# A spectral filter and a GEGLU block, forward and backward: the first W sums in two stretches, transposes a step earlier, the tail first in its step, a third Vt slot

## The chip, the cores and the metric

The kernel runs on one core of a Trainium2 chip. The metric is the device time of one execution in microseconds, as the median of several runs. A separate execution was recorded by the hardware profiler. All traces and rows below come from that one.

PE is the tensor engine (matmul), DVE the vector engine, ACT the scalar engine, POOL the GpSimd engine, and SP the engine whose queue issues most DMAs. PSUM is the memory into which PE writes its sums.

## The reference, cut to what matters

```python
x = A_x                                   # 2048 x 576
g = sigmoid((x * gate_w).sum(-1, keepdims=True))
a = irfft2(rfft2(x) * (A_w_r + 1j * A_w_i))
b = (gelu(x @ W_gate) * (x @ W_up)) @ W_down      # 576 -> 4608 -> 576
out = g * a + (1 - g) * b
# returned: out, and for a given grad_out the gradients of
# x, A_w_r, A_w_i, W_gate, W_up, W_down and gate_w
```

All inputs and outputs are bf16. The forward product `b` is needed as well as its gradients, so every intermediate of the GEGLU block is formed once and used several times.

## The kernel before, in words

**Layout.** The 2048 rows of x and of grad_out are held as 16 row tiles of 128 rows. `xn` and `dB` hold them by rows, `xT` and `dOT` transposed. The 4608 hidden columns are cut into 18 groups of 256 (`FG`). The first stage loops over groups `g` and, inside, over `m` = 0 to 3, each `m` being four row tiles. One pass of the inner loop is called a step here, numbered `pr` = 4g + m (0 to 71).

**What one step does.** `H_mm` makes z = dOT x W_down^T (lines 402 and 407) and the two 64-row parts of xy (line 411). The inner function `full` adds the main part of xy = xT x [W_gate, W_up] (line 418) for two row tiles at a time. ACT evacuates z as `da` (L430) and xy as `xb`, `q` and `hu` (L437 to L440). On DVE, `H_ew1` computes the first half of the elementwise work (L445 to L447). `H_ew2` (called through `sigs`) has two sigmoids on ACT (L461, L462) and eight DVE products (L466 to L473) that end in the tiles `A`, `dHu` and `dHg`, 128 x 4 x 256 each. They are stored to DRAM for the second stage and also kept in SBUF.

**W sums.** When a group is through all its 16 row tiles, its weight gradients are summed over them during the next group's four steps. `W_units(g)` returns five lists of closures with a weight in us each: four lists for the four steps, and one that is carried into the step after. `w[0]` to `w[3]` are the gradients of W_gate (k = 1, from `dHg`, `w[0]` and `w[1]`) and W_up (k = 2, from `dHu`), each over 256 of the 576 rows in two halves `cc` of 16 matmuls (L525). `tail` is the last 64 rows of both (L538). `d[0]` to `d[3]` are the gradient of W_down, two halves of 8 matmuls each (L508). Each sum needs one `wps` tile, and there are two such PSUM tiles (pool `pw`). The finished sum is copied out by `wevac` (L486), through ACT or, while `wcopy` is DVE's copy, through DVE. It lands in a stage tile (`dw`, `dwt` or `dwd`, two slots each) and is stored by POOL's DMA queue.

**The spectral part.** The transforms are cut into small units in a list `fft`. `want(pr)` says how many of them should have been issued after each step. The table `FIRST` gives this for steps 0 to 7, and from there the rest is spread evenly up to step 65. In a step with n new units, the first sits inside the second half of xy, and the others at points of the W closures where the sum of weights passes a value of `spots`. A unit that finds no such point is issued after the last closure. Units and `z` share one PSUM tile (pool `pz`, one buffer): a unit's matmuls write it, ACT evacuates it, and then the next unit or the next z may write. A forward unit of the first kind is six matmuls (L568), of the second kind two (L585). The second kind and the middle units end in a tile `Vt` of the pool `half` (two slots), stored by an SP DMA (L592, L771).

**Tables.** `build_R` (DVE, L164 and L165), `columns_B` (DVE L180 to L182, then POOL L186 and L189) and `build_B` (POOL iotas L216 to L220, later DVE L225 to L231) prepare tables. Their sines are run on ACT by `run_late` in two steps (`tables`), and in those steps the W sums that come later are copied out by DVE. `scale_dB` scales `dB` in place on DVE (L946) before the `d` sums use it.

**The first group.** For g = 0 nothing is left over from a group before. Instead, the row tiles are transposed by PE as they are needed. `titems` returns three closures per source and per four row tiles: eight, eight and four transposes (L367 and L373) into a PSUM tile `pg` (two buffers), each followed by a copy into `dOT` or `xT` (L374). `gate` computes the sigmoid gate (L383 to L387) and uses a `pg` buffer too. `held` delays the second elementwise half of a step into the next step.

**Order.** The schedule is manual: each engine executes its instructions in the order in which the program text issues them. An instruction that waits holds everything behind it on its engine.

**The second stage**, from about 960 us, reads the stored tiles back transposed and forms `b` and the gradient of x (L1140).

Of the kernel before, what the change touches and what calls it, by code (L numbers as in the profile page):

```python
# [11 lines left out]
BF16 = mybir.dt.bfloat16  # L12
# [8 lines left out]
P, T = 128, 16  # L21
# [9 lines left out]
FG = 256  # L31
TPB = 512 // FG
# [212 lines left out]
def kernel(  # L245
# [4 lines left out]
    nc = tc.nc  # L250
# [7 lines left out]
    unit = Unit(ctx.enter_context(tc.tile_pool(name="unit", bufs=NUNIT, side="right")), "unit")  # L258
    hstack = ExitStack()
    hres = hstack.enter_context(tc.tile_pool(name="hres", bufs=1, side="right"))  # L260
    half = Unit(hstack.enter_context(tc.tile_pool(name="half", bufs=2, side="right")), "half")
    wpool = hstack.enter_context(tc.tile_pool(name="wpool", bufs=2, side="right"))

    wstack = ExitStack()
# [220 lines left out]
    def wevac(out, in_):  # L485
        wcopy[0](out, in_)  # L486

    def W_units(g):
        fsl = slice(g * FG, (g + 1) * FG)
        kt = kept[g]  # L490

        def tl(k, t):
            return kt[t // 4][k][:, t % 4, :]
        dwd_tiles, wp = {}, {}

        def halves(f, us):
            return [(us, lambda: f(0)), (us, lambda: f(1))]

        def wtile(key):
            if key not in wp:  # L500
                wp[key] = pw.tile([P, TPB, FG], F32, tag="wps", name="wps")
            return wp[key]

        def u_dwd(fch, h):
            def f(half):
                wps = wtile(("d", fch, h)).rearrange("p a b -> p (a b)")
                for t in range(8 * half, 8 * half + 8):
                    nc.tensor.matmul(wps[:, :288], lhsT=tl(0, t)[:, fch * P:(fch + 1) * P],  # L508
                                     rhs=dB[:, t, h * 288:(h + 1) * 288], start=(t == 0), stop=(t == T - 1))
                if half == 0:  # L510
                    return
                if h == 0:
                    dwd_tiles[fch] = stage.tile([P, D], BF16, tag="dwd", name="dwd")
                dwd = dwd_tiles[fch]
                wevac(dwd[:, h * 288:(h + 1) * 288], wps[:, :288])
                if h == 1:
                    r0 = g * FG + fch * P
                    wst[0].dma_start(out_6[r0:r0 + P, :], dwd[:])
            return halves(f, 1.0)

        def u_dw(k, ov, c0):
            def f(cc):
                wps = wtile(("w", k, c0))
                for t in range(T):
                    nc.tensor.matmul(wps[:, cc, :], lhsT=xn[:, t, (c0 + cc) * P:(c0 + cc + 1) * P],  # L525
                                     rhs=tl(k, t), start=(t == 0), stop=(t == T - 1))
                if cc == 0:
                    return
                dw = stage.tile([P, TPB, FG], BF16, tag="dw", name="dw")
                wevac(dw[:], wps[:])  # L530
                wst[0].dma_start(ov[:, c0:c0 + TPB, fsl], dw[:])  # L531
            return halves(f, 1.7)

        def tail():
            wps = wtile("t")
            for t in range(T):
                for k, r in ((1, LO), (2, HI)):
                    nc.tensor.matmul(wps[r, 0, :], lhsT=xn[:, t, 512:576], rhs=tl(k, t),  # L538
                                     start=(t == 0), stop=(t == T - 1))
            dw = stage.tile([P, FG], BF16, tag="dwt", name="dwt")  # L540
            wevac(dw[:], wps[:, 0, :])
            wst[0].dma_start(out_4[512:576, fsl], dw[LO, :])
            wst[0].dma_start(out_5[512:576, fsl], dw[HI, :])
        tl_ = [(2.0, tail)]
        w = [u_dw(k, ov, c0) for k, ov in ((1, o4v), (2, o5v)) for c0 in range(0, 4, TPB)]
        d = [u_dwd(fch, h) for fch in range(FCH) for h in range(2)]
        if g == 0:
            return [[w[0], tl_], [w[1], d[0]], d[1:], [w[2]], w[3]]
        return [[d[0]], [d[1], d[2], d[3]], [w[0], tl_], [w[1], w[2]], w[3]]


    side = []
# [356 lines left out]
    mid_at = 4 * T + 10  # L909
    NPR = NT // 2  # L910
    LASTP = NG * NPR - 7
    FIRST = (0, 0, 0, 0, 0, 3, 5, 9)
    done = [0]

    def want(pr):
# [22 lines left out]

    wgT_from = 54

    carry, pend, held = [], None, []
    scaled = [0]

    def scale_dB(n):
# [4 lines left out]
    for g in range(NG):  # L949
# [3 lines left out]
        for m in range(NPR):  # L953
            pr = g * NPR + m
            n = want(pr) - done[0]
            done[0] += n
            hs = [h for u in pend[m] for h in u] if pend else []

            def side_work(us):
                while side and us > 0:  # L960
                    us -= side[0][0]
                    side.pop(0)[1]()
            tiles = [ewt(tag, g) for tag in ("xb", "q", "hu")]
            state = []

            def sigs(m=m, tiles=tiles, state=state):
                H_ew2(g, m, tiles, state[0], state[1])
            if g == 0:
                pgs3 = (pgtile,) * 3
                if m < NPR - 1:  # L970
                    t1 = 4 * m + 4
                    cp = ((VC, VC, VC), (VC, VC, VC)) if m == 0 else ((VC, VC, AC), (AC, VC, VC))
                    its = titems(dB, dOT, t1, pgs3, cp[0]) + titems(xn, xT, t1, pgs3, cp[1])
                else:
                    its = []
                z, xy_full = H_mm(g, m, [lambda: gate(0)] if m == 0 else its[:2])
                da = H_da(g, m, z)
                if m > 0:
                    for f in its[2:]:
                        f()  # L980
                if held:
                    held.pop()()
                xy = xy_full(0)
                if m == 0:
                    for f in its:
                        f()
                    build_R(nc, tb, unit, 4)
                    columns_B(nc, tb, res)
                    next(makeB)
                for part in (1, 0):  # L990
                    H_act(0, xy, tiles, part)
                xy = xy_full(1)
                for part in range(2):
                    H_act(1, xy, tiles, part)
                if m < NPR - 1:
                    gate(m + 1)
                state += [H_ew1(g, tiles), da]
                if m < NPR - 1:
                    held.append(sigs)
                else:  # L1000
                    V.tensor_copy(g32[:], g_bf[:])
                    V.tensor_scalar(gs32[:], g32[:], SD2, None, op0=ALU.mult)
                    sigs()
            else:
                z, xy_full = H_mm(g, m)
                xy = xy_full(0)
                da = H_da(g, m, z)
                for part in (1, 0):
                    H_act(0, xy, tiles, part)
                xy = xy_full(1, fft_next if n else None)  # L1010
                for part in range(2):
                    H_act(1, xy, tiles, part)
                state += [H_ew1(g, tiles), da]
                if pr == 4:
                    scale_dB(12)
                elif pr == 5:
                    scale_dB(4)
                    build_R(nc, tb, unit, 8)
                    build_R(nc, tb, unit, 12)
                elif pr == 6:  # L1020
                    next(makeB)
                side_work(4.4)
                at, k = 0.0, min(n, 1)
                spots = (0.0, 1.6, 3.6) if n < 4 else (0.0, 1.0, 2.6, 4.2, 5.0, 5.0)
                tables = pr in (4, 6)
                for w, f in carry + hs:
                    if k < n and at >= spots[k - (n == 2)]:
                        fft_next()
                        k += 1
                    if tables and k == n:  # L1030
                        run_late(tb)
                        wcopy[0] = VC
                        tables = False
                    if pr == NG * NPR - 1 and at == 0.0:
                        sigs()
                    f()
                    at += w
                wcopy[0] = AC
                while k < n:
                    fft_next()  # L1040
                    k += 1
                flush()
                if pr < NG * NPR - 1:
                    sigs()
            carry = []
            if m < 3 and g + 1 < NG:
                load_w(g + 1, m)
            if done[0] == n_slots or (pr >= wgT_from and pr % 2 == 0 and len(wgT_all) < 20):
                load_wgT()
                if done[0] == n_slots:  # L1050
                    load_wgT()
# [243 lines left out]
```

## Time and profile before

| what | value |
|---|---|
| median of 3 runs | 1433.06 us (1432.56 to 1434.38) |
| the profiled execution | 1435.61 us |
| its span, first to last instruction | 1433.8 us |
| mean granted clock of PE | 0.994 |
| PE busy | 1380.7 us (96%) |
| DVE busy / ACT busy | 735.9 us (51%) / 731.4 us (51%) |
| POOL busy | 222.6 us (16%) |
| start of z in steps 1, 2, 3, 4 | 20.39, 30.80, 44.22, 50.28 us |
| start of z in steps 5, 6, 7, 8 | 70.73, 84.00, 98.99, 112.43 us |

How to read the rows: a timeline row gives start, duration, engine, line and operation, output <- inputs, tile shape and how many instructions were merged, and in brackets how long the engine had been idle before it and what released it. A row of waits gives who waited for whom, the total, how often and the longest. In the 40 slices of the page a digit is the busy share in tenths. PEclk is the clock that PE was granted, in tenths of full speed.

### The profile page before, as it was taken

Reading aid. Unit: us, or ns where it says so; the run is one execution under the profiler, and the core shown is the slowest. Engines: PE = TensorE matmul, PEld = TensorE weight load, DVE = VectorE, ACT = ScalarE, POOL = GpSimd, SP = SyncE. Lnnn points to the kernel's source line nnn. Section 1 sums busy time; section 2 is a strip of 40 time slices with the busy share of each in tenths; the row PEclk is TensorE's granted clock in tenths of the full one; section 3 lists DMA queues with packets and bytes.
Section 4 is the critical chain, followed back from the end, with each engine's and each line's share of the span. In section 5 each row is a group of like instructions: output and inputs, shape, how many; then the busy total and the mean of one; then the engine's idle time right before and its main releaser. Section 6 shows DMA issues by size and latency. Waiting matters only on the chain.

```text
span 1433.8 us, 28098 instructions
## 1 busy us (share of the span) xinstructions
PE 1380.7 (96%) x11357; PEld 1026.5 (72%) x11430; DVE 735.9 (51%) x1403; ACT 731.4 (51%) x1324; POOL 222.6 (16%) x420
## 2 busy tenths in 40 slices
PE   8799999999999899999999999999999999999997
PEld 6466766766766666667767676768777777777775
DVE  7775656464887688784665656551000642212100
ACT  6777777677778788777677777662000000000000
POOL 3000010122344236330100010110000100000000
PEclk9899999999999999999999999999999999999999
DMA  6333344445564565555356554859999997788772
GB/s 210 96 85 110 107 120 120 120 124 151 130 162 126 138 162 141 143 149 155 104 155 166 132 154 131 179 128 228 212 193 198 235 202 167 157 159 167 157 155 61
DMA packets 509534, 214.62 MB, mean 150 GB/s; under 512 B 311418, under 2 KB 502588, under 8 KB 509404
## 3 DMA queue, kind: packets, MB, share of 16 engines
q1 hardware_dynamic: 493402, 187.44, 55.8%
q0 software_dynamic: 13872, 24.24, 6.2%
q8 instruction: 89, 1.46, 0.5%
q10 hardware_dynamic: 2130, 1.15, 0.3%
q14 instruction: 41, 0.34, 0.1%
HBM read 41.05 MB, written 93.84 MB: 94 GB/s over the span
## 4 chain that ended last, share of the span: by engine, by line
PE 92%; ACT 3%; DVE 2%; DMA 1%; issue 1%; SPq 0%; ACTq 0%; DVEq 0%
PE acc L1140 29%; PE wps L525 18%; PE xy L418 16%; PE z L402 9%; PE wps L508 9%; PE wps L538 2%; PE xy L411 2%; PE pf L568 2%; PE z L407 2%; PE pf L838 1%; PE pf L840 1%; PE pf L677 1%; PE pf L766 1%; PE pf L812 1%; PE pf L585 1%
## 5 line engine op out<-in xcount | busy, mean ns | idle before, releaser
L1140 PEld LDWEIGHTS <-pin 128*128 128x128 bf16 x3456 | 337.7, 98 | 86.3 <-DMA pin<-scr 1.1
L418 PE MATMUL xy<-wgu,xT 128*128 128x512 bf16 x1079 | 257.7, 381 | 10.3 <-issue 9.6
L525 PEld LDWEIGHTS <-xn 128*128 128x128 bf16 x2304 | 225.7, 98 | 44.2 <-issue 6.1
L418 PEld LDWEIGHTS <-xT 128*128 128x128 bf16 x1152 | 106.8, 98 | 138.4 <-issue 31.7
L1157 ACT COPY bo<-acc 128x288 f32<-128x288 f32 x32 | 12.8, 399 | 305.0 <-PE acc L1140 305.0
L466 DVE TENSOR_TENSOR xb<-xb,s 128x1024 bf16<-128x1024 bf16 x72 | 49.8, 692 | 216.0 <-ACT s L462 216.0
L508 PE MATMUL wps<-dB,A 128*128 128x288 bf16 x1152 | 154.8, 286 | 1.9 <-DVE dwd L486 1.9
L402 PE MATMUL z<-wdT,dOT 128*128 128x256 bf16 x1152 | 137.5, 272 | 13.5 <-ACT ev L844 3.0
L1140 PE MATMUL acc<-wgT,pin 128*128 128x288 bf16 x1152 | 143.8, 286 | 0.0
L1140 PE MATMUL acc<-wuT,pin 128*128 128x288 bf16 x1152 | 143.6, 286 | 0.1
L1140 PE MATMUL acc<-wd_all,pin 128*128 128x288 bf16 x1152 | 142.9, 286 | 0.1
L525 PE MATMUL wps<-dHg,xn 128*128 128x256 bf16 x1152 | 137.0, 275 | 5.8 <-DVE dHg L473 5.8
L525 PE MATMUL wps<-dHu,xn 128*128 128x256 bf16 x1152 | 135.8, 273 | 0.0
L508 PEld LDWEIGHTS <-A 128*128 128x128 bf16 x1152 | 112.0, 98 | 32.7 <-issue 2.1
L402 PEld LDWEIGHTS <-dOT 128*128 128x128 bf16 x1152 | 111.4, 98 | 32.9 <-issue 19.1
L531 POOL DMA_DIRECT2D out_dram<-dw x67 | 49.2, 734 | 513.1 <-ACT dw L486 418.5
L430 ACT ACTIVATE da<-z,omg 128x256 bf16<-128x256 f32 x288 | 112.2, 471 | 12.0 <-PE z L407 11.9
L439 ACT CAST xb<-xy 128x512 bf16<-128x512 f32 x144 | 85.2, 592 | 35.0 <-PE xy L418 35.0
L1217 DVE SCALAR_TENSOR_TENSOR f32t<-gwf,dlog,b16t 128x576 f32<-128x576 f32 x16 | 13.1, 818 | 171.4 <-DMA b16t<-dxa_scr 171.4
L437 ACT ACTIVATE q<-xy 128x512 bf16<-128x512 f32 x144 | 88.1, 614 | 8.7 <-PE xy L418 6.8
L486 ACT CAST dw<-wps 128x512 bf16<-128x512 f32 x71 | 41.6, 586 | 90.9 <-PE wps L525 86.8
L440 ACT CAST hu<-xy 128x512 bf16<-128x512 f32 x144 | 87.3, 606 | 0.0
(212 smaller groups left out, 1698.7 us busy)
## 6 DMA issues: line engine op xcount, KB each, us to landing
scr<-A SPq DMA_DIRECT2D x72, 256.0 KB, 2.8
scr<-dHg SPq DMA_DIRECT2D x72, 256.0 KB, 2.9
scr<-dHu SPq DMA_DIRECT2D x72, 256.0 KB, 3.5
out_dram<-dw POOLq DMA_DIRECT2D x67, 128.0 KB, 2.3
wd_all<-in_B_w_down_dram SPq DMA_DIRECT2D x3, 1728.0 KB, 15.9
out_dram<-dwd POOLq DMA_DIRECT2D x34, 144.0 KB, 3.0
scr_p<-Vt SPq DMA_DIRECT2D x32, 145.0 KB, 2.7
wgu<-in_B_w_gate_dram SPq DMA_DIRECT2D x18, 256.0 KB, 4.0
```

The source lines that it names most:

```text
L402: nc.tensor.matmul(zo(t), lhsT=dOT[:, ci, t, :], rhs=wdT[:, ci, :], start=(t % 4 < 2 and ci == 0), stop=False)
L418: nc.tensor.matmul(xy[k][:, t % 2, :], lhsT=xT[:, ci, t, :], rhs=wgu[:, ci, :], start=False, stop=(ci == 3))
L430: nc.scalar.activation(da[:, t, :], z[:, t % 2, t // 2, :], ACT.Copy, scale=omg32[:, 4 * m + t:4 * m + t + 1])
L437: nc.scalar.activation(q[:, h, :], xy[:, :, 0:FG], ACT.Square)
L439: nc.scalar.copy(xb[:, h, :], xy[:, :, 0:FG])
L440: nc.scalar.copy(hu[:, h, :], xy[:, :, FG:2 * FG])
L466: V.tensor_tensor(xb[:], xb[:], s[:], op=ALU.mult)
L486: wcopy[0](out, in_)
L508: nc.tensor.matmul(wps[:, :288], lhsT=tl(0, t)[:, fch * P:(fch + 1) * P], rhs=dB[:, t, h * 288:(h + 1) * 288], start=(t == 0), stop=(t == ...
L525: nc.tensor.matmul(wps[:, cc, :], lhsT=xn[:, t, (c0 + cc) * P:(c0 + cc + 1) * P], rhs=tl(k, t), start=(t == 0), stop=(t == T - 1))
L531: wst[0].dma_start(ov[:, c0:c0 + TPB, fsl], dw[:])
L1140: nc.tensor.matmul(acc[:, :288], lhsT=src[:, r, :], rhs=w_of(r)[:, h * 288:(h + 1) * 288], start=(first and r == 0), stop=(last and r == F ...
```

## The change

- For group 0, the two W_gate sums `w[0]` and `w[1]` are cut at row tile 12: all four stretches over row tiles 0 to 11 are issued in step 4, the four over row tiles 12 to 15 in step 5. Both `wps` tiles stay open in between. In every other group a sum is cut into quarters of 8 matmuls in the same order as before, so that weights are 0.85 instead of 1.7.
- Step 5 also takes the tail of group 0, ahead of `d[0]`. In the later groups the tail goes ahead of `w[0]` in its step. Its stage tile now has the tag `dw` and shares those two slots.
- In group 0, the transposes of dB's row tiles 8 to 11 move from step 1 into step 0, and those of dB's row tiles 12 to 15 from step 2 into the end of step 1 (the last of the three closures into step 2's z). Those of xn stay in their steps, after `da`. Which copies go to ACT and which to DVE changes too.
- The second elementwise half of step 3 is held into step 4, between the first and the second evacuation of xy.
- `build_R(4)` moves from step 0 to step 4, `columns_B` and the first part of `build_B` from step 0 to step 5, `build_R(8)` and `build_R(12)` from step 5 to steps 6 and 7, and the sines from steps 4 and 6 to steps 5 and 7. `scale_dB` does 8 and 8 row tiles in steps 4 and 5 instead of 12 and 4.
- `FIRST` is (0, 0, 0, 0, 0, 0, 3, 5) instead of (0, 0, 0, 0, 0, 3, 5, 9).
- The pool `half` has three slots.

```diff
-    half = Unit(hstack.enter_context(tc.tile_pool(name="half", bufs=2, side="right")), "half")
+    half = Unit(hstack.enter_context(tc.tile_pool(name="half", bufs=3, side="right")), "half")
...
-        def u_dw(k, ov, c0):
-            def f(cc):
+        def u_dw(k, ov, c0, cut=T // 2):
+            both = cut != T // 2
+
+            def f(cc, t0, t1):
                 wps = wtile(("w", k, c0))
-                for t in range(T):
+                for t in range(t0, t1):
                     nc.tensor.matmul(wps[:, cc, :], lhsT=xn[:, t, (c0 + cc) * P:(c0 + cc + 1) * P],
-                                     rhs=tl(k, t), start=(t == 0), stop=(t == T - 1))
-                if cc == 0:
+                                     rhs=tl(k, t), start=(t == 0 and (cc == 0 or not both)),
+                                     stop=(t == T - 1 and (cc == 1 or not both)))
+                if cc == 0 or t1 < T:
                     return
...
-            return halves(f, 1.7)
+            parts = [(cc, t0, t1) for cc in range(TPB) for t0, t1 in ((0, cut), (cut, T))]
+            if both:
+                parts.sort(key=lambda a: a[1])
+            return [(1.7 * (a[2] - a[1]) / T, lambda a=a: f(*a)) for a in parts]
...
-            dw = stage.tile([P, FG], BF16, tag="dwt", name="dwt")
+            dw = stage.tile([P, TPB, FG], BF16, tag="dw", name="dwt")
...
         if g == 0:
-            return [[w[0], tl_], [w[1], d[0]], d[1:], [w[2]], w[3]]
-        return [[d[0]], [d[1], d[2], d[3]], [w[0], tl_], [w[1], w[2]], w[3]]
+            return [[w[0][:2], w[1][:2]], [w[0][2:], w[1][2:], tl_, d[0]], d[1:], [w[2]], w[3]]
+        return [[d[0]], [d[1], d[2], d[3]], [tl_, w[0]], [w[1], w[2]], w[3]]
...
-    FIRST = (0, 0, 0, 0, 0, 3, 5, 9)
+    FIRST = (0, 0, 0, 0, 0, 0, 3, 5)
...
+                def items(src, dst, t, *cp):
+                    return titems(src, dst, 4 * t, (pgtile,) * 3, cp)
+                head_, early, mid_, late_ = [
+                    ([lambda: gate(0)], [], items(dB, dOT, 1, VC, VC, VC) + items(xn, xT, 1, VC, VC, VC) + items(dB, dOT, 2, AC, AC, VC), []),
+                    ([], items(xn, xT, 2, VC, VC, VC), [], items(dB, dOT, 3, AC, AC, VC)),
+                    ([], items(xn, xT, 3, VC, VC, VC), [], []),
+                    ([], [], [], [])][m]
+                if m == 1:
+                    rest.append(late_.pop())
+                elif m == 2:
+                    head_ = [rest.pop()]
+                z, xy_full = H_mm(g, m, head_)
...
-                if m < NPR - 1:
-                    held.append(sigs)
                 else:
                     V.tensor_copy(g32[:], g_bf[:])
                     V.tensor_scalar(gs32[:], g32[:], SD2, None, op0=ALU.mult)
-                    sigs()
+                for f in late_:
+                    f()
+                state += [H_ew1(g, tiles), da]
+                held.append(sigs)
             else:
...
                 for part in (1, 0):
                     H_act(0, xy, tiles, part)
+                if held:
+                    held.pop()()
                 xy = xy_full(1, fft_next if n else None)
...
+                if pr in (4, 5):
+                    scale_dB(T // 2)
                 if pr == 4:
-                    scale_dB(12)
+                    build_R(nc, tb, unit, 4)
                 elif pr == 5:
-                    scale_dB(4)
+                    columns_B(nc, tb, res)
+                    next(makeB)
+                elif pr == 6:
                     build_R(nc, tb, unit, 8)
+                    next(makeB)
+                elif pr == 7:
                     build_R(nc, tb, unit, 12)
-                elif pr == 6:
-                    next(makeB)
...
-                tables = pr in (4, 6)
+                tables = pr in (5, 7)
```

More of the change, by code (lines that the diff above doesn't have):

```diff
@@ L539, in tail @@
                                      start=(t == 0), stop=(t == T - 1))
-            dw = stage.tile([P, FG], BF16, tag="dwt", name="dwt")
-            wevac(dw[:], wps[:, 0, :])
-            wst[0].dma_start(out_4[512:576, fsl], dw[LO, :])
-            wst[0].dma_start(out_5[512:576, fsl], dw[HI, :])
+            dw = stage.tile([P, TPB, FG], BF16, tag="dw", name="dwt")
+            wevac(dw[:, 0], wps[:, 0, :])
+            wst[0].dma_start(out_4[512:576, fsl], dw[LO, 0, :])
+            wst[0].dma_start(out_5[512:576, fsl], dw[HI, 0, :])
         tl_ = [(2.0, tail)]
-        w = [u_dw(k, ov, c0) for k, ov in ((1, o4v), (2, o5v)) for c0 in range(0, 4, TPB)]
+        w = [u_dw(k, ov, c0, 12 if g == 0 and k == 1 else T // 2) for k, ov in ((1, o4v), (2, o5v)) for c0 in range(0, 4, TPB)]
         d = [u_dwd(fch, h) for fch in range(FCH) for h in range(2)]
         if g == 0:
-            return [[w[0], tl_], [w[1], d[0]], d[1:], [w[2]], w[3]]
-        return [[d[0]], [d[1], d[2], d[3]], [w[0], tl_], [w[1], w[2]], w[3]]
+            return [[w[0][:2], w[1][:2]], [w[0][2:], w[1][2:], tl_, d[0]], d[1:], [w[2]], w[3]]
+        return [[d[0]], [d[1], d[2], d[3]], [tl_, w[0]], [w[1], w[2]], w[3]]
     side = []
@@ L939 @@
     wgT_from = 54
-    carry, pend, held = [], None, []
+    carry, pend, held, rest = [], None, [], []
     scaled = [0]
@@ L964, with sigs @@
             state = []
-            def sigs(m=m, tiles=tiles, state=state):
+            def sigs(g=g, m=m, tiles=tiles, state=state):
                 H_ew2(g, m, tiles, state[0], state[1])
             if g == 0:
-                pgs3 = (pgtile,) * 3
-                if m < NPR - 1:
[L971 to L976, printed above, removed]
+                def items(src, dst, t, *cp):
[10 more added lines that the diff above has]
+                z, xy_full = H_mm(g, m, head_)
                 da = H_da(g, m, z)
-                if m > 0:
-                    for f in its[2:]:
-                        f()
+                for f in early:
+                    f()
                 if held:
@@ L983 @@
                 xy = xy_full(0)
[L984 to L988, printed above, removed]
-                    next(makeB)
+                for f in mid_:
+                    f()
                 for part in (1, 0):
@@ L996 @@
                     gate(m + 1)
-                state += [H_ew1(g, tiles), da]
-                if m < NPR - 1:
-                    held.append(sigs)
                 else:
@@ L1002 @@
                     V.tensor_scalar(gs32[:], g32[:], SD2, None, op0=ALU.mult)
-                    sigs()
+                for f in late_:
+                    f()
+                state += [H_ew1(g, tiles), da]
+                held.append(sigs)
             else:
@@ L1013 @@
                 state += [H_ew1(g, tiles), da]
+                if pr in (4, 5):
+                    scale_dB(T // 2)
                 if pr == 4:
-                    scale_dB(12)
+                    build_R(nc, tb, unit, 4)
                 elif pr == 5:
-                    scale_dB(4)
+                    columns_B(nc, tb, res)
+                    next(makeB)
+                elif pr == 6:
                     build_R(nc, tb, unit, 8)
+                    next(makeB)
+                elif pr == 7:
                     build_R(nc, tb, unit, 12)
-                elif pr == 6:
-                    next(makeB)
                 side_work(4.4)
```

## The prediction

> **What bounds the kernel now.** I read four views in this order: the page, the tensor engine's (PE) waits, PE's timeline beside the granted clock in 2 us windows, and the vector engine's (DVE) timeline. "Step n" is n = 4g + m of the group loop, and step n begins at its z product.
>
> ```profile
> PE 1380.7 (96%) x11357; PEld 1026.5 (72%) x11430; DVE 735.9 (51%) x1403; ACT 731.4 (51%) x1324; POOL 222.6 (16%) x420
> ...
> PE   8799999999999899999999999999999999999997
> ...
> DVE  7775656464887688784665656551000642212100
> ...
> PEclk9899999999999999999999999999999999999999
> ```
>
> PE is busy for 1380.7 of 1433.8 us, so the sum is about 53 us of PE idleness, and about the half-clock time hidden in "busy". The change leaves every matmul in place. The first slices are the weak ones, DVE is at seven tenths there, and the second clock digit is an 8.
>
> ```profile
> PE wps L525 <- DVE dHg L473: 5.8, 1, 5.8
> ...
> PE z L402 <- ACT Vt L769: 2.4, 1, 2.4
> PE z L402 <- ACT ve L588: 2.2, 3, 0.8
> ...
> PE pf L373 <- DVE dOT L374: 2.0, 2, 1.7
> PE wps L508 <- DVE dwd L486: 1.9, 1, 1.9
> ```
>
> (Waiting line <- releaser: total us, times, longest.) The largest is step 4's W sum waiting for the last quarter of dHg. PE's timeline around it, and around the transposes of step 2:
>
> ```profile
> 36.05 0.38 PE L373 MATMUL pf<-ident,dB 128*128 128x128 bf16 x4 [1.69 <-DVE dOT L374]
> ...
> 38.35 0.41 PE L373 MATMUL pf<-ident,xn 128*128 128x128 bf16 x4 [0.64 <-ACT xT L374]
> 38.99 4.89 PE L418 MATMUL xy<-wgu,xT 128*128 128x512 bf16 x15 [0.22 <-issue]
> ...
> 47.04 3.40 PE L418 MATMUL xy<-wgu,xT 128*128 128x512 bf16 x15 [0.16 <-issue]
> ...
> 64.13 4.42 PE L525 MATMUL wps<-dHg,xn 128*128 128x256 bf16 x20 [5.76 <-DVE dHg L473]
> ```
>
> The same 15 matmuls take 4.89 us after the waits and 3.40 a step later. The windows say why (the last three columns are granted clock, DMA share and GB/s):
>
> ```profile
> 40.00:42.00 2.00, 2.00 (x7) 0.63 (x5) 1.55 (x3) 0.35 (x1) 0.00 (x0) 0.50 0.00 0
> ...
> 66.00:68.00 2.00, 2.00 (x11) 1.40 (x10) 2.00 (x9) 1.99 (x2) 0.00 (x0) 0.50 0.93 247
> ```
>
> Both waits are followed by half clock (0.50). So a wait here costs itself plus what runs at half speed after it.
>
> **Part 1, the transposes (steps 0 to 2).** Eight transposes are 0.53 us, four 0.26 (1.06 for 16, L367). Each block needs one of two pg buffers, freed by a copy: DVE 0.69 us, ACT 1.01. Step 0 gains dB's row tiles 8 to 11: 20 transposes = 1.3 us, plus a wait of 0.2 for the buffer and 0.7 for the ACT copy: PE +2.2. ACT's two copies (2.0) go ahead of the first evacuation of step 0, and that is hidden: step 1's 64-row xy matmuls need it only 4 us later. Step 1 does 36 transposes for 40 (-0.3), and its waits of 0.86 + 0.31 become about 0.25 for a DVE copy and 0.6, because the gate's buffer is freed only by an ACT sigmoid behind the evacuations: -0.6. Step 2 does 24 for 40 (-1.06), loses the waits 1.69 + 0.21 (at 36.65) + 0.64 for one of 0.25 (-2.3), and the half clock goes (4.89 - 3.40 = -1.5): -4.9. At the start of step 3 PE stands at +2.2 - 0.6 - 4.9 = -3.3; with small waits in a crowded stage I take **-3.0**.
>
> [...] The rows show half clock after no single wait above 1.69 us (2.54 in three). [...]
>
> build_R(4), columns_B and the first table iotas also leave step 0. That is 1.56 (L164, L165) + 1.1 us (L180 to L182) of DVE, which puts the following elementwise work that much earlier.
>
> **Part 2, step 4.** The first 12 row tiles need only quarters 0 to 2. 48 matmuls at 0.109 us (16 in 1.75 before the next starts) = 5.2 us replace w[0] and the tail (3.5 + 1.76 = 5.26): equal work. The 5.76 us wait goes, and so does the half clock behind it: 20 matmuls took 4.36 to the next start, not 2.18, and the tail 2.24, not 1.8: 2.6. A wait of 0.4 for hu stays (0.6 now, ACT does step 2's sigmoids first). At the start of step 5: -3.0 - 5.76 - 2.6 + 0.3 = **-11**.
>
> **Part 3, what is late next: step 5.** Both wps buffers stay held from step 4, and the tail needs a third accumulator, so PE stops until w[0] is copied out. That copy is on DVE (this is now the table step, so wcopy is DVE) at the end of a queue:
>
> ```profile
> 58.80 0.69 DVE L466 TENSOR_TENSOR xb<-xb,s 128x1024 bf16<-128x1024 bf16 x1 [1.58 <-ACT s L462]
> ...
> 63.39 0.69 DVE L473 TENSOR_TENSOR dHg<-hu,om 128x1024 bf16<-128x1024 bf16 x1
> ...
> 65.47 3.44 DVE L946 TENSOR_SCALAR dB<-dB,omg 128x576 bf16<-128x576 bf16 x12
> ```
>
> One step's second elementwise half is 58.80 to 64.0 (5.3), its first half 64.0 to 65.47 (1.47), a dB tile 0.28. After: the second half of step 3 starts near 57.5 (now behind ACT's work of step 4), then 5.3 + 1.47 + 8 dB tiles 2.3 + build_R 1.55 + step 4's 5.3 + 1.47 + 8 tiles 2.3 + columns_B 1.1 = 20.8: the copy runs from 78.3 to 79. PE is there at 70.73 - 11 + 6.2 (z, xy) + 1.75 (16 matmuls) = 67.7. It waits **10.9 us**, and the half clock that follows costs 2 (about 4 us of work at half speed). No forward units run in step 5 now (before: two first, one second = 1.75; the rest, 5.5, is equal). Start of step 6: -11 - 1.75 + 10.9 + 2 = **+0.2**. So nearly everything that step 4 gives is handed back: DVE is the bound from step 3 to 5.
>
> Behind that copy, POOL has the 20 columns_B and iota instructions in front of the store of w[0] (21.70 to 27.44 in the trace, 5.7 us), and the tail's dw tile waits for that store, since it now shares the two dw slots. DVE stands until about 87. PE needs the tail's wps buffer in step 6 only near 91, so 4 us of slack cover it.
>
> **Steps 6 and 7.** dwd's 1.88 us wait (a table step before) goes, and step 6 runs three units for two: -1.1. Step 7 runs two for four (-1.0), both early in the step, so its two waits of 0.79 at 111.24 and 112.43, each for a unit's evacuation, go: -2.6. Start of step 8: 0.2 - 1.1 - 2.6 = **-3.5**.
>
> **Part 4, the body.** The forward units skipped up to step 8 are four (9 - 5): two firsts at 0.75, two seconds at 0.25 = 2.0 us, done later: **+2.0**. Tail first: with the old order the weights before the third unit are 1.7, 3.4, and only after the tail 5.4, past the spot at 3.6. So the unit comes last, and the next z (one buffer) waits for its evacuation:
>
> ```profile
> 150.41 0.91 PE L568 MATMUL pf<-Dt,xT 128*128 128x290 bf16 x6
> ...
> 153.12 0.42 PE L585 MATMUL pf<-Y,Rt 128*128 128x290 bf16 x2
> ...
> 154.28 1.91 PE L402 MATMUL z<-wdT,dOT 128*128 128x256 bf16 x16 [0.73 <-ACT ve L588]
> ```
>
> With 2.0 first and quarters of 0.85, the spots fall at 2.0 and 3.7, with 1.75 us of matmuls behind, more than the 0.64 us copy. In the timeline seven tail steps show this wait (154, 211, 270, 689, 745, 802, 858 us): 0.73 to 1.1 each, 6.0 in all: **-6.0**. The shifted slots make other units end a step: half of the other z and pf waits (about 5 us) might double or vanish; I take **+1.5**, with -1 and +5 as ends. Quarters instead of halves in w cost nothing on PE (same matmuls, same order).
>
> Third Vt slot: one wait, 2.42 us, after a store of 5.82 us against a median of 2.7 for scr_p:
>
> ```profile
> 463.39 5.82 DMA scr_p<-Vt
> ...
> 470.17 1.91 PE z L402 x16
> ```
>
> With three slots the copy waits for the store of three units earlier, at 2.3 us a unit 6.9 us, more than 5.82: **-2.4** (0 if that store was slow by chance in this execution, and no other is).
>
> **Sum**: -3.5 + 2.0 - 6.0 + 1.5 - 2.4 = **-8.4 us**. The profiled execution took 1435.61 us (span 1433.8 and 1.8 around it), 2.55 above the median of the runs, 1433.06. I carry the difference over: 1433.06 - 8.4 = **1424.7 us**. The last stage (from 960 us) has PE at 50.00 of 50 us and is untouched.
>
> **The rivals.** (B) The waits only move: units end other steps, the store at 463 was chance. Then the tail gives 2 and the slot 0: -8.4 + 4 + 2.4 = -2.0 us, 1431. For: the other waits of this kind (ten of them) are in steps without a tail. Against: the spots after the change leave 1.75 us behind the unit. [...] (D) Slower: the POOL chain of step 5. If POOL's table instructions and the store of w[0] take longer than 5.7 + 2.3 us, the tail's copy is late, DVE's whole queue behind it too, and PE stops in step 6 for the tail's wps buffer. The first 4 us are slack, then each costs one. From 12 us too late on (POOL at three times its rows) nothing is left of the 8.4; at 15 it is +3, 1436. For: its L189 rows go up to 0.67 us beside DVE, against 0.19 alone. Against: DVE stands idle in just that stretch. [...]
>
> **How the numbers follow.** This measurement tells about 0.2% (2.9 us): faster is below 1430.2, slower above 1435.9. Likeliest case -5 to -11.5: 0.62. B, -5 to 0: 0.19, half of it beyond 0.2%. C: 0.11. D and any other new wait: 0.08. Faster 0.62 + 0.11 + 0.10 = 0.83, same 0.09, slower 0.08. The range takes C's edge and most of B: 1420 to 1431.5.
>
> **What would show it.** Right: no wait on dHg in PE's list; a new one of about 11 us at the tail for DVE's dw copy near 68 to 79 us, half clock behind it and none before it; z of step 3 near 41; no z wait directly behind a tail step; no Vt wait near 465. Wrong: step 6 starting over 3 us later than 84.0, z waits in the body still above 10 us, or DVE and POOL still late at step 8.

## The result and the profile after

The changed kernel takes 1425.43 us (median of 4 runs, 1424.87 to 1426.35) against 1433.26 us (median of 4 runs, 1432.56 to 1434.38). The ratio is 0.9945, with a 95% interval of 0.9928 to 0.9962: 7.8 us faster, beyond the 0.2% that this measurement can tell from no change. The forecast was 1424.7 us, 8.4 below the kernel before. The profiled execution took 1425.01 us, with a span of 1423.2 us and a mean granted clock of 0.994, the same clock as before.

The page of the changed kernel, the same rows as before (busy time, then busy tenths and granted clock in 40 slices):

```profile
PE 1378.3 (97%) x11357; PEld 1026.5 (72%) x11430; DVE 733.8 (52%) x1403; ACT 729.9 (51%) x1324; POOL 223.0 (16%) x420
...
PE   8879999999999999999999999999999999999997
...
DVE  6866556464698778885565656551000642112100
...
PEclk9989999999999999999999999999999999999999
```

PE runs the same 11357 matmuls. The 8 in the clock row is no longer in the second slice but in the third: the stretch at half clock moved instead of vanishing. The waits of PE in the changed kernel (total us, times, longest) say where:

```profile
PE wps L544 <- DVE dw L486: 11.0, 1, 11.0
...
PE z L402 <- ACT ev L850: 1.5, 2, 0.8
...
PE pf L574 <- ACT da L430: 1.2, 1, 1.2
...
PE z L402 <- ACT ve L594: 0.8, 1, 0.8
PE xy L411 <- ACT hu L440: 0.8, 1, 0.8
...
PE pf L367 <- ACT g_bf L385: 0.8, 1, 0.8
```

The 5.8 us for dHg are gone, and a single wait of 11.0 us stands in their place, the tail waiting for DVE's copy of dw. No z waits for Vt any more. PE's timeline from step 2 to step 6 of the changed kernel (start, duration, what, and in brackets the idle time before it):

```profile
36.58 0.38 PE L373 MATMUL pf<-ident,xn 128*128 128x128 bf16 x4 [0.33 <-DVE xT L374]
37.02 3.40 PE L418 MATMUL xy<-wgu,xT 128*128 128x512 bf16 x15
...
53.88 5.40 PE L527 MATMUL wps<-dHg,xn 128*128 128x256 bf16 x48
59.12 1.91 PE L402 MATMUL z<-wdT,dOT 128*128 128x256 bf16 x16
...
65.18 1.91 PE L527 MATMUL wps<-dHg,xn 128*128 128x256 bf16 x16
78.11 0.37 PE L544 MATMUL wps<-dHg,xn 128*64 128x256 bf16 x1 [11.02 <-DVE dw L486]
...
81.67 2.60 PE L508 MATMUL wps<-dB,A 128*128 128x288 bf16 x16
84.11 1.91 PE L402 MATMUL z<-wdT,dOT 128*128 128x256 bf16 x16
```

The 15 xy matmuls of step 2 now take 3.40 us instead of 4.89. The 48 matmuls on row tiles 0 to 11 run without a wait. Then PE stands from 67.1 to 78.1 us, and the first work after it is slow, with the granted clock at 0.50 up to 82.6 us: the `d[0]` sum takes 2.60 us where a later one takes 2.12. What PE waited for is at the end of DVE's queue:

```profile
56.89 0.69 DVE L466 TENSOR_TENSOR xb<-xb,s 128x1024 bf16<-128x1024 bf16 x1 [2.71 <-ACT s L462]
...
73.94 2.32 DVE L952 TENSOR_SCALAR dB<-dB,omg 128x576 bf16<-128x576 bf16 x8
...
77.37 1.28 DVE L486 CAST dw<-wps 128x512 bf16<-128x512 f32 x2
85.20 0.42 DVE L486 CAST dwt<-wps 128x256 bf16<-128x256 f32 x1 [6.55 <-DMA out_dram<-dw]
```

From 56.89 to 78.65 DVE has no gap. The copy `dwt` after it waits 6.55 us for the store of `w[0]`, and PE does not feel this.

The starts of z, read from PE's timeline of both kernels, place the gain:

| z of step | before, us | after, us | difference | forecast |
|---|---|---|---|---|
| 1 | 20.39 | 22.35 | +1.96 | +2.2 |
| 3 | 44.22 | 40.76 | -3.46 | -3.0 |
| 5 | 70.73 | 59.12 | -11.61 | -11 |
| 6 | 84.00 | 84.11 | +0.11 | +0.2 |
| 8 | 112.43 | 108.37 | -4.06 | -3.5 |
| 71 | 958.76 | 950.30 | -8.46 | -8.4 |

The profiled spans differ by 10.6 us, 2.1 more than at step 71. Those 2.1 are in the stage after it, which the change does not touch; most of it (1.45) lies behind the last matmul, where the last stores land. The medians (-7.8) do not show it, and it is not counted as an effect.

### The profile page after: what moved, and what is told of

Read it like the earlier page. It is cut to its first block, busy times and chain, and to the rows that moved or that the text cites. A ratio compares the mean times of both kernels' runs of the same rounds, so it can differ in the third digit from the quotient of the medians.

```text
span 1423.2 us, 28073 instructions
## 1 busy us (share of the span) xinstructions
PE 1378.3 (97%) x11357; PEld 1026.5 (72%) x11430; DVE 733.8 (52%) x1403; ACT 729.9 (51%) x1324; POOL 223.0 (16%) x420
## 4 chain that ended last, share of the span: by engine, by line
PE 91%; ACT 4%; DVE 3%; issue 1%; DMA 0%; ACTq 0%; SPq 0%; DVEq 0%
PE acc L1151 30%; PE wps L527 16%; PE xy L418 15%; PE wps L508 10%; PE z L402 8%; PE wps L544 2%; PE xy L411 2%; PE pf L574 2%; PE z L407 1%; PE pf L844 1%; PE pf L683 1%; PE pf L846 1%; PE pf L591 1%; PE pf L818 1%; PE pf L772 1%
```

## The experiments

All four ran together, with 18 runs of the kernel before beside them (median 1433.0 us). "Step n at x" below is the start of z of step n against the profiled execution of the kernel before. One execution is enough for a wait but not for half a microsecond: the first two kernels, in which PE's order is that of the kernel before up to step 9, stand at -0.5 and -0.9 there.

**Tail first alone.** The kernel before, with the sums in quarters and the tail ahead of `w[0]`:

```diff
-            return halves(f, 1.7)
+            parts = [(cc, t0, t1) for cc in range(TPB) for t0, t1 in ((0, T // 2), (T // 2, T))]
+            return [(0.85, lambda a=a: f(*a)) for a in parts]
...
-        return [[d[0]], [d[1], d[2], d[3]], [w[0], tl_], [w[1], w[2]], w[3]]
+        return [[d[0]], [d[1], d[2], d[3]], [tl_, w[0]], [w[1], w[2]], w[3]]
```

> The kernel before with two edits alone: from group 1 on the tail goes ahead of w[0] in its step, and w sums are issued in quarters of 8 matmuls. My theory (a unit that was issued last in a tail step now has 1.75 us of matmuls behind it, so the next z no longer waits for its evacuation): the seven tail-step waits of 0.73 to 1.1 us go, 6.0 us less, 5 to 6 with shifted slots, nothing before step 8. Rival (the waits only move to other steps): z waits as before in total, time within 2 us of before.

Measured: 1428.19 us, ratio 0.9967 (0.9955 to 0.9980), 4.8 us faster. The difference between the two starts of z changes by more than 0.3 us in eight of the steps behind step 8. Seven of these are those behind the seven tail steps named in the prediction, by -0.75 to -0.89 each, -5.9 in all. The eighth, step 34, has -1.4: in this execution the Vt wait was 1.0 us instead of 2.4. Around the first of the seven, this kernel's timeline of PE has

```profile
149.27 0.91 PE L569 MATMUL pf<-Dt,xT 128*128 128x290 bf16 x6
150.01 1.91 PE L525 MATMUL wps<-dHg,xn 128*128 128x256 bf16 x16
151.76 0.41 PE L586 MATMUL pf<-Y,Rt 128*128 128x290 bf16 x2
152.01 1.03 PE L525 MATMUL wps<-dHg,xn 128*128 128x256 bf16 x8
```

and the next z at 152.90 without a bracket, where the kernel before had 0.73 us. Eight matmuls (0.9 us) now lie behind the last unit, and here that is enough to cover its evacuation (0.64 us in the kernel before, L588). Behind two of the seven steps 0.23 us of the wait stay (z at step 59 and 63, waiting for `ZT`). By the trace, the 6.0 of the sum was near the truth for the old count of units; the medians give 4.8.

**The third Vt slot alone.** The kernel before, with three slots in `half`. Room for them comes as in the change, from `dwt` sharing the slots of `dw`:

```diff
-    half = Unit(hstack.enter_context(tc.tile_pool(name="half", bufs=2, side="right")), "half")
+    half = Unit(hstack.enter_context(tc.tile_pool(name="half", bufs=3, side="right")), "half")
...
-            dw = stage.tile([P, FG], BF16, tag="dwt", name="dwt")
+            dw = stage.tile([P, TPB, FG], BF16, tag="dw", name="dwt")
```

> The kernel before with a third Vt slot alone (the tail's stage tile shares the dw slots, to make room). My theory: the one wait of 2.4 us near 465 us goes, 2.4 us less. Rival (that store was slow by chance in the profiled execution, others of its kind take 2.7 us): no Vt wait in most executions of either kernel, time within 0.5 us of before.

Measured: 1429.56 us, ratio 0.9977 (0.9968 to 0.9985), 3.4 us faster. The difference stays at -0.9 up to step 30, is -3.5 at step 34 and stays there to step 71. So the slot gives 2.6 us in one place. The chain in the kernel before is in ACT's waits between 455 and 471 us:

```profile
ACT Vt L769 <- DMA scr_p<-Vt: 3.3, 1, 3.3
```

In the kernel with three slots neither this wait nor the z wait behind it exists. It was no chance of one execution: the same wait was there again, at 1.9 us, in the profiled execution of the tail-first kernel. The timelines of ACT and SP in the kernel before show what made the store late, besides its own 5.82 us. Three Vt were due in one step (460.89, 463.67 and, after the wait, 469.31 us). The first was complete at 461.73, but SP was issuing eight loads of `wgu` and `Vp` one after the other from 458.09 on, and came to the store only at 463.39.

**The rest alone.** The changed kernel with the old tail order, sums in halves again outside the cut ones, and two Vt slots. What is left is the new order of group 0 and the new `FIRST`:

```diff
-    half = Unit(hstack.enter_context(tc.tile_pool(name="half", bufs=3, side="right")), "half")
+    half = Unit(hstack.enter_context(tc.tile_pool(name="half", bufs=2, side="right")), "half")
...
-            parts = [(cc, t0, t1) for cc in range(TPB) for t0, t1 in ((0, cut), (cut, T))]
+            parts = [(cc, t0, t1) for cc in range(TPB) for t0, t1 in (((0, cut), (cut, T)) if both else ((0, T),))]
...
-        return [[d[0]], [d[1], d[2], d[3]], [tl_, w[0]], [w[1], w[2]], w[3]]
+        return [[d[0]], [d[1], d[2], d[3]], [w[0], tl_], [w[1], w[2]], w[3]]
```

> The changed kernel with the old order of the tail, whole halves and two Vt slots: what the edits to the first eight steps and FIRST give alone. By the sum in the prediction (-3.5 at step 8, +2.0 for the units done later): 1.5 to 3 us less than before. Rival (the new FIRST shifts which step issues which unit, and with the tail last more units end a step): step 8 about 3.5 us earlier all the same, but the body gives it back and more, 3 to 7 us slower than before.

Measured: 1437.38 us, ratio 1.0031 (1.0020 to 1.0042), 4.4 us slower. My sum had a gain here and fell; the rival was right. Up to step 8 this kernel does what the changed one does (step 8 at -3.9). Then it loses 7.4 us up to step 71, where it stands at +3.5. The four deferred units are 2.0 of this, by the prediction's figure. PE's waits show most of the rest: the z waits are 15.0 us behind step 8 in all (12.3 in the kernel before, 2.4 of them the Vt wait), and the waits of the units' own matmuls (`pf`) are 5.7 (3.5 before), 1.2 of them at step 8 for `da`. The z waits are:

```profile
PE z L402 <- ACT Xg L688: 2.8, 2, 1.4
PE z L402 <- ACT ev L850: 2.3, 3, 0.8
PE z L402 <- ACT ZT L821: 2.2, 2, 1.1
PE z L402 <- ACT Xx L688: 2.2, 3, 1.4
PE z L402 <- ACT ve L594: 1.5, 2, 0.7
...
PE z L402 <- ACT RT L636: 1.1, 1, 1.1
```

Of the 15.0 us, 11.5 stand directly behind twelve tail steps; in the kernel before it was 6.0 behind seven. One of the added ones, in the timelines of this kernel, of the kernel before and of the changed kernel, at the same z (step 27):

```profile
376.33 0.42 PE L683 MATMUL pf<-Vp,Btab 128*128 128x289 bf16 x2
378.12 1.91 PE L402 MATMUL z<-wdT,dOT 128*128 128x256 bf16 x16 [1.38 <-ACT Xg L688]
```

```profile
376.63 0.27 PE L538 MATMUL wps<-dHu,xn 128*64 128x256 bf16 x1
376.84 1.92 PE L402 MATMUL z<-wdT,dOT 128*128 128x256 bf16 x16
```

```profile
371.89 0.41 PE L683 MATMUL pf<-Vp,Btab 128*128 128x289 bf16 x2
372.13 1.91 PE L527 MATMUL wps<-dHg,xn 128*128 128x256 bf16 x16
373.88 1.91 PE L402 MATMUL z<-wdT,dOT 128*128 128x256 bf16 x16
```

With the new count and the old order, a middle unit falls into the last place of the step and z waits 1.38 us. Before, that step had no unit at its end. With the tail first, sixteen matmuls lie behind the unit. So with four units fewer at step 8, a unit stands at the end of five more tail steps. In the changed kernel, with the tail first and its sums in quarters, most of that loss is gone. The three parts are not additive: alone they give -4.8, -3.4 and +4.4, -3.8 in all, and together -7.8.

One more thing is missing in this kernel: ACT's wait for a store of Vt. It has two slots, and no such wait. Its stores of Vt in that stretch are no quicker (5.2 us from issue to landing for the one that the trace has), but with the shifted count only two Vt are made close together (467.38 and 469.19 us), and the third not before 476.89.

**The sums uncut.** The changed kernel with `w[0]` and `w[1]` of group 0 not cut at row tile 12 and in their old steps, and with the tail of group 0 back in step 4; everything else stays:

```diff
-        w = [u_dw(k, ov, c0, 12 if g == 0 and k == 1 else T // 2) for k, ov in ((1, o4v), (2, o5v)) for c0 in range(0, 4, TPB)]
+        w = [u_dw(k, ov, c0, T // 2) for k, ov in ((1, o4v), (2, o5v)) for c0 in range(0, 4, TPB)]
...
-            return [[w[0][:2], w[1][:2]], [w[0][2:], w[1][2:], tl_, d[0]], d[1:], [w[2]], w[3]]
+            return [[w[0], tl_], [w[1], d[0]], d[1:], [w[2]], w[3]]
```

> The changed kernel with group 0's two W_gate sums not cut at row tile 12: lists as before (w[0] and tail in step 4, w[1] and d[0] in step 5), quarters of 8, everything else as changed. Theory A (the cut is worth what it removed, 5.8 us of wait and 2.6 of half clock): about 8 us slower than the changed kernel. Theory B (the cut only moves the wait, DVE sets when step 6 can go on, and with the cut a third sum waits for a copy at the end of DVE's queue and a store behind POOL's table work): a wait for dHg of about 8 us in step 4, none at the tail in step 5, step 6 starting 3 to 5 us earlier than in the changed kernel, and the whole 3 to 5 us faster than it.

Measured: 1422.55 us, ratio 0.9923 (0.9912 to 0.9935), 10.5 us faster than the kernel before, and the fastest of all. Against the changed kernel it was not timed in the same runs; by the two medians it is 2.9 us faster, while the intervals of the two ratios just overlap (0.9912 to 0.9935, 0.9928 to 0.9962). The traces carry the reading. PE's largest wait, and its timeline, in this kernel:

```profile
PE wps L527 <- DVE dHg L473: 6.9, 1, 6.9
```

```profile
54.45 1.47 PE L527 MATMUL wps<-dHg,xn 128*128 128x256 bf16 x12
62.80 4.43 PE L527 MATMUL wps<-dHg,xn 128*128 128x256 bf16 x20 [6.88 <-DVE dHg L473]
...
79.23 2.31 PE L508 MATMUL wps<-dB,A 128*128 128x288 bf16 x16
81.38 1.91 PE L402 MATMUL z<-wdT,dOT 128*128 128x256 bf16 x16
```

The old wait is back and 1.1 us longer than before, since PE is earlier. But it is one wait of 6.9 us in place of one of 11.0. Step 6 stands at -2.6 instead of +0.1, step 8 at -6.8 instead of -4.1, and from there to step 71 the two kernels move alike (-4.37 and -4.40). So the cut, with the tail's move to step 5 that goes with it, costs 2.7 us, all of it before step 6. (In this execution the uncut kernel was 0.57 us behind the changed one at step 4, so steps 4 and 5 alone differ by 3.3.) The reason is in ACT's timeline of the uncut kernel:

```profile
67.27 0.58 ACT L486 CAST dw<-wps 128x512 bf16<-128x512 f32 x1 [8.38 <-PE wps L527]
69.77 0.37 ACT L486 CAST dwt<-wps 128x256 bf16<-128x256 f32 x1 [1.92 <-PE wps L544]
```

Uncut, `w[0]` and the tail end in step 4, where ACT copies them out as soon as they are complete. Cut, both accumulators stay open into step 5, where the copies go to DVE and stand behind two steps of elementwise work, and the tail needs a third accumulator there. Which share the cut has in the 2.7 us and which the tail's place was not separated.

**What was not run.** Four things stay open. The tail moved on into step 6 with the sums still cut, which would show whether the cut pays once nothing needs a third accumulator in step 5. POOL's table work in step 5 made longer, which is rival D. The old count of units from step 8 on with the old tail order, which would test directly that the count alone makes the loss of the third experiment. And the changed kernel with two Vt slots.

## Why the prediction was right, and where it was not

**Part 1, the transposes: right.** +1.96 for +2.2 in step 0, -0.40 for -0.6 in step 1, -5.02 for -4.9 in step 2. The gate's buffer cost 0.78 us for 0.6. The half clock of step 2 went with the waits: with those of 1.69 and 0.64 us gone, the clock was 1.00 in each window of 0.5 us from 34 to 72 us, and xy took 3.40 us. The 1.5 us were there to be won. All three kernels with the old step 2 (before, tail first, third slot) have 3.41 us at half clock there, and none of the three with the new one.

**Part 2, step 4: right.** -11.61 for -11. The small term was short: the wait for hu was to grow by 0.3 in the sum, and went from 0.38 to 0.82 us.

**Part 3, step 5: right in size.** 11.02 us for 10.9, with the copy at 77.37 instead of 78.3 and PE there at 67.1 instead of 67.7. The forecast's own times (79 less 67.7) give 11.3, so 10.9 was a slip of 0.4 us; with it put right the sum is -8.0. The 2 us for the half clock behind the wait were an estimate; half clock fell on 4.5 us of work there (78.1 to 82.6), which makes about 2.3. Step 6 at +0.11 for +0.2 says that DVE's queue, not PE's work, set the end of this stretch. The sentence "nearly everything that step 4 gives is handed back" held, and the uncut kernel shows it was even too kind: cut, with the tail in step 5, the kernel lost 2.7 us against not cutting. The prediction compared the new order only with the kernel before, not with the same edit without its first part.

**Steps 6 and 7: right.** Step 8 at -4.06 for -3.5. One wait was not foreseen: in step 8 the first unit waits 1.18 us for ACT's `da` (L574). It lies behind the z of step 8, and so in the next term.

**Part 4, the body: right in sum, wrong in its terms.** From step 8 to step 71 the forecast was -4.9 (+2.0 - 6.0 + 1.5 - 2.4) and -4.40 was measured. The waits of the two kernels behind step 8 give the terms:

| term | forecast, us | by the waits, us |
|---|---|---|
| z waits behind tail steps, 5.97 to 2.05 | -6.0 | -3.9 |
| Vt wait | -2.4 | -2.4 |
| other z waits (3.93 to 2.31) and unit waits (3.5 to 4.6) | +1.5 | -0.5 |

With the 2.0 of the deferred units the waits give -4.8, and 0.4 us stay without a name. Two terms missed by 2 us each, in opposite directions: that the sum came out was luck.

The tail term rested on a wrong reading of the spots. The prediction says that 1.75 us of matmuls lie behind the last unit. That holds for a step with three units; the step it shows has four, whose last spot is at 4.2, and there the trace has eight matmuls, 0.9 us, which still cover the copy. In a step with five units, however, one comes last all the same: z waits 0.85 and 0.74 us behind two such tail steps (z at step 19 and 55), 1.6 of the 2.05 us that are left. Two more keep 0.23 us. So the sign "no z wait directly behind a tail step" was not met: four are left.

The third experiment shows how the terms hang together. It has +7.41 from step 8 to step 71 without the tail order, the quarters and the slot. Taking the deferred units' 2.0 off, the shift of the units cost 5.4 us net on the old order, outside the ends of -1 and +5 that the forecast gave its +1.5. Tail first, quarters and the slot together then gave 11.8 us (7.41 + 4.40), and 9.5 of it stand behind tail steps (11.5 to 2.05). The sum priced the tail's order on the old places of the units and the shift of the units apart from it, though the change made both at once.

**The third slot.** The -2.4 was right for the kernel before (-2.6 alone). In the changed kernel it is probably counted twice in my sum: with the new count, in the third experiment, that wait was already gone with two slots. What the slot still gives beside the tail's new order was not run.

**The rivals.** B, that the waits only move, is excluded by the total z waits behind step 8: 12.3 us before, 4.4 after, while the units' own waits rose only from 3.5 to 4.6. Its mechanism is real, though. It is what the third experiment does. C, a larger gain at the start, with the range's lower end of 1420 us as its edge, did not come in this kernel: step 8 was only 0.6 better than the sum. The uncut kernel came nearer to that edge, with 1422.55 us, by its order of the sums. D, the POOL chain of step 5, did not decide: POOL's table work took 5.0 us (77.64 to 82.6) for the 5.7 estimated, and the tail's copy ran at 85.20, for "near 87". PE had no wait for its buffer. Where its slack ends was not tried.

## What to carry to other kernels

When a wait on the busiest engine is filled with other work, find what that work keeps open, and which engine has to release it in which step. A sum that is cut holds its accumulator for the whole gap, and here the release landed at the end of DVE's queue, behind two steps of work; the uncut order, with the tail a step earlier, was 2.9 us faster by the medians. Where two edits move the same things (a count of units and the order around them), price them together on the new places: the edits that gave 4.8 us faster and 4.4 us slower alone gave 7.8 us faster with the third.

## What the runs showed of the hardware

Read in windows of 0.5 us from 20 to 130 us, the kernel before had one stretch at half clock (0.50) of 3.41 us and one of 6.83, the changed kernel one of 10.24 us, and the uncut kernel one of 10.24 us: once, twice and three times the shortest. The changed kernel's windows of 2 us (after the length come the busy times of PE, PEld, DVE, ACT and POOL; the last three columns are granted clock, DMA share and GB/s):

```profile
72.00:74.00 2.00, 0.00 (x0) 0.00 (x0) 1.90 (x5) 1.99 (x3) 0.00 (x0) 0.60 0.22 62
...
80.00:82.00 2.00, 2.00 (x19) 1.53 (x16) 0.00 (x0) 0.00 (x0) 1.76 (x7) 0.50 0.00 0
82.00:84.00 2.00, 2.00 (x16) 1.46 (x15) 0.00 (x0) 0.00 (x0) 1.99 (x6) 0.84 0.00 0
```

So the clock fell at 72.4 us, 5.3 us after PE stopped at 67.1, and rose at 82.6, 4.5 us after it had work again. In the kernel before, half clock came after much shorter waits: the stretch of 3.41 us followed waits of at most 1.69 us, 2.54 in three, and up to then PE had no longer wait than that 1.69 us.

Nor did the wait alone set where the stretch began. Three kernels have the old step 2, with the 1.69 us wait ending at 36.05 us (before), 36.28 (tail first) and 36.12 (third slot). In windows of 0.5 us their half clock began at 38.6, 37.7 and 37.3 us, so 2.5, 1.4 and 1.2 us after it. In each of these executions the second stretch began 23.9 us after the first.

The total at half clock from 20 to 130 us is the same 10.24 us before and after. What it cost depends on how much of it fell on work: about 3.2 + 5.2 us of matmul time before (in step 2, and from 64.13 to 69.3), 4.5 us after. In the changed kernel 5.7 us of the 10.24 lay within the wait of 11.02 us. In the kernel before 1.7 us of the 6.83 lay within the wait of 5.76 us, and of the 3.41 us behind the short waits of step 2 all but 0.2 fell on work.
